# Summing seven taps on TensorE: row tiles with a short stream in place of column tiles

## The chip, the cores and the metric

The kernel runs on one core of a Trainium2 chip. Times are device microseconds (us) of one execution. The kernel before takes 418.44 us, the median of 3 runs (417.84 to 418.45); its profiled execution spans 416.7 us.

## What is computed

The input `x` has 8 sequences of 4160 tokens with 192 channels. Each token has, for each of 8 heads (24 channels), 7 weights. They go through a softmax, and each channel of the token becomes the weighted sum of that channel over the token and the six before it. The result goes through a layer of 1024 hidden values, each the larger of two products, and back to 192 channels.

```python
w = np.exp(weight_gen - max)                       # over the 7 taps
w = w / (np.sum(w, axis=-1, keepdims=True) + 1e-09)
out = np.einsum('bshk,bskhg->bshg', w, x_unf)      # x_unf: the token and the 6 before it
...
h1 = x @ w1                                        # 192 -> 1024
h2 = x @ w2
g = np.maximum(h1, h2)
return (g @ w_out).astype(np.float32)              # 1024 -> 192
```

## The kernel before

The 33280 tokens are laid on 128 partitions, 260 on each. Position number c on all partitions together, 128 tokens, is called a column here. Columns go in batches of 16, and each batch in pieces: four of 4 columns in the first two batches, two of 8 later. The first 32 columns are thus eight units of 4 columns.

For each piece ScalarE makes the softmax weights in bf16, each one twice, in the order tap, token, head:

```python
def weights(b, o):
    N = dict(pieces(b))[o] * H                     # 4 columns x 8 heads = 32
    ...
    nc.scalar.activation(
        out=_sub(en_ts[b], o * WGC * 2, [[2 * N, K], [2, N], [1, 2]]),
        in_=_sub(wg_ts[b], o * WGC, [[1, K], [K, N], [0, 2]]), func=AF.Exp,
    )
```

VectorE multiplies all seven taps of a piece in one instruction. The tile `m_t` then holds seven stretches (taps) of 4 x 192 products for each partition:

```python
def mul(b, o):
    n = dict(pieces(b))[o]
    nc.vector.tensor_tensor(
        out=m_t[:, K * o * D:K * (o + n) * D],
        in0=_sub(xb_ts[b], o * D, [[D, K], [1, n * D]]),
        in1=_sub(en_ts[b], o * WGC * 2, [[2, K * n * H], [0, G // 2], [1, 2]]),
        op=ALU.mult,
    )
```

For later columns VectorE adds up the taps and a DMA transposes the sum, so that channels stand on partitions. In the first 32 columns TensorE does both at once. Each product takes a block of `m_t` as its weights and the identity as its stream, which transposes the block, and the products of the taps add up in PSUM. In five of the eight units VectorE has added three pairs of taps before, so that four are left (`LEFT`); in three units all seven are summed here.

```python
def sum_transpose(u, taps=range(K)):
    b, o, n = UNITS[u]
    nb = n // 2 * 3                                # 6 blocks
    yps = ps[...].tile([P, 1024], FP32, name="yps", tag="op")
    for k in range(nb):
        for t in taps:
            for j in range(2):
                at = (K * o + t * n + k // 3 + j * n // 2) * D + k % 3 * 64
                nc.tensor.matmul(
                    yps[half(j), k * P:(k + 1) * P], lhsT=m_t[:, at:at + 64],
                    rhs=ident, start=(t == taps[0]), stop=(t == taps[-1]), skip_group_check=True,
                )
    yt = pyt.tile([P, 8 // 2 * 3 * P], BF16, name="yt", tag="yt")
    nc.scalar.copy(out=yt[:, 0:nb * P], in_=yps[:, 0:nb * P])
    yt_ts[u] = yt
```

A product has 128 tokens x 64 channels as weights and 128 columns of the identity as its stream. The two products `j` go to the two halves of the PSUM partitions: two column tiles of the array.

The result `yt` feeds the hidden layer (`hid_tile`, weights `wd`, tile `hdp` or `hd`), whose products have 64 rows and 128 columns, two row tiles. ScalarE rectifies it to bf16 (`relu`, tile `rd_t`), and the output products (`op_ps`) follow in two passes (`out_first`, with the terms of `yt` in it, and `out_second`). ScalarE copies their result to `o_t` (`evac`). An empty instruction on ScalarE's queue (`relay`) waits for the first pass and lets the second one start. A group is worked through like this:

```python
def hidden(g, now=(), between=lambda: None, beside=lambda: None):
    ...
    for t in range(t0, t0 + n - 1):
        hid_tile(t)
    if now:
        out_room(now, ...)
        last = out_first(now)
    ...                                            # relu of the first tiles
    if now:
        go = relay(last)
    hid_tile(t0 + n - 1)
    ...
    relu(rd, t0 + n - 1, 1)
    between()                                      # in groups 4 to 7: a sum_transpose
    if now:
        out_second(now, go)
        evac(now[0] // 2, len(now) // 2)
```

The eight sums stand in this order among other work: units 0 and 1 around the first groups, unit 2 before the fourth, unit 3 after it, each behind ScalarE's and VectorE's work of the opening; units 4 to 7 in groups 4 to 7. The pieces of weights of the first batch are made in a row at the start, those of the second batch in two pairs, ahead of the copy of unit 2 and behind that of unit 3.

Of the kernel before, what the change touches and what calls it, by code (L numbers as in the profile page):

```python
# [12 lines left out]
AF = mybir.ActivationFunctionType  # L13
# [4 lines left out]
def _sub(base: bass.AP, off: int, dims):  # L18
    ap = [list(base.ap[0])] + [[int(s), int(c)] for s, c in dims]
    return dataclasses.replace(base, offset=base.offset + off, ap=ap)  # L20
# [3 lines left out]
def kernel(  # L24
# [9 lines left out]
    nc = tc.nc  # L34

    B, S, D = x.shape
    H, K = weight_gen.shape[2], weight_gen.shape[3]
    F = moe_w1.shape[1]
    P = 128
    PAD = K - 1  # L40
    WGC = H * K
# [11 lines left out]
    def pieces(b):  # L53
        n = BATCHES[b][1]
        at, done = [], 0
        for w in (4, 4, 4, 4) if b < 2 else (8, 8) if n == 16 else (n,):
            at.append((done, w))
            done += w
        return at
# [38 lines left out]
    wg_ts, xb_ts, e_ts, s_ts, en_ts, y_ts, yt_ts = {}, {}, {}, {}, {}, {}, {}  # L98

    m_t = pm.tile([P, K * 16 * D], BF16, name="m_t")  # L100
# [48 lines left out]

    def weights(b, o):  # L150

        N = dict(pieces(b))[o] * H
        if b not in en_ts:
            en_ts[b] = pen.tile([P, 16 * WGC * 2], BF16, name="en_t", tag="en")
        nc.scalar.activation(  # L155
            out=_sub(en_ts[b], o * WGC * 2, [[2 * N, K], [2, N], [1, 2]]),
            in_=_sub(wg_ts[b], o * WGC, [[1, K], [K, N], [0, 2]]), func=AF.Exp,
        )


    def mul(b, o):

        n = dict(pieces(b))[o]
        nc.vector.tensor_tensor(  # L164
            out=m_t[:, K * o * D:K * (o + n) * D],
            in0=_sub(xb_ts[b], o * D, [[D, K], [1, n * D]]),
            in1=_sub(en_ts[b], o * WGC * 2, [[2, K * n * H], [0, G // 2], [1, 2]]),
            op=ALU.mult,
        )
# [44 lines left out]
    def half(j):  # L214
        return slice(64 * j, 64 * j + 64)
# [4 lines left out]
    def sum_transpose(u, taps=range(K)):  # L220

        b, o, n = UNITS[u]
        nb = n // 2 * 3
        yps = ps["r" if "r" in ps else "o"].tile([P, 1024], FP32, name="yps", tag="op")
        for k in range(nb):
            for t in taps:
                for j in range(2):
                    at = (K * o + t * n + k // 3 + j * n // 2) * D + k % 3 * 64
                    nc.tensor.matmul(  # L229
                        yps[half(j), k * P:(k + 1) * P], lhsT=m_t[:, at:at + 64],  # L230
                        rhs=ident, start=(t == taps[0]), stop=(t == taps[-1]), skip_group_check=True,
                    )
        yt = pyt.tile([P, 8 // 2 * 3 * P], BF16, name="yt", tag="yt")
        nc.scalar.copy(out=yt[:, 0:nb * P], in_=yps[:, 0:nb * P])
        yt_ts[u] = yt


# [143 lines left out]
    for g in range(3, len(GROUPS)):  # L381
        most = 4 if g == 3 else 2 if GROUPS[g][1] == 2 or len(OUTS[-1]) == 4 else 4
        n = min(most, ready[g] - c)
# [75 lines left out]
    ident = consts.tile([P, P], BF16, name="ident")  # L459
# [4 lines left out]
    with tc.tile_pool(name="pstage", bufs=1) as pstage:  # L464
# [7 lines left out]
        for p0, p1, eng in ((16, P, nc.sync), (1, 16, nc.gpsimd)):  # L472
            eng.dma_start(
                out=xs[p0:p1, 0:PAD * D],
                in_=bass.AP(tensor=x.tensor, offset=(p0 * CPP - PAD) * D,
                            ap=[[CPP * D, p1 - p0], [1, PAD * D]]),
# [38 lines left out]
        for o in (0, 4, 8, 12):  # L515
            weights(0, o)
        nc.vector.tensor_copy(out=xb_ts[0][:, PAD * D:(PAD + 4) * D],
                              in_=xs[:, PAD * D:(PAD + 4) * D])
        mul(0, 0)
        nc.scalar.copy(out=xb_ts[0][:, (PAD + 4) * D:(PAD + 8) * D], in_=xs[:, (PAD + 4) * D:])  # L520
        w1 = {kind: pstage.tile([nr, F], BF16, name="w1" + kind)
              for kind, nr in (("E", P), ("T", 64))}

        def w_diff(h, copy):
# [15 lines left out]
            out=wo[:, :].rearrange("p (f d) -> p f d", d=D),  # L540
            in_=bass.AP(tensor=moe_w_out.tensor, offset=0, ap=[[D, P], [P * D, FCH], [1, D]]),
# [29 lines left out]
        keep_warm(115)  # L571
        w_diff(0, nc.scalar.copy)
        sum_transpose(0)
        keep_warm(14)
        mul(0, 4)


        nc.scalar.copy(out=w1["E"], in_=ws["E", 0])
        hidden(0)
        nc.scalar.copy(out=w1["T"], in_=ws["T", 0])  # L580
        w_diff(1, nc.vector.tensor_copy)
        mul(0, 8)
        adds(0, 8, True)
        sum_transpose(1)
        exp_sum(1)
        red(1)
# [24 lines left out]
        for h in range(2):  # L611
            nc.scalar.copy(out=w1t[:, 4 * h * D:4 * (h + 1) * D], in_=tp[:, h * 1024:h * 1024 + 4 * D])
        weights(1, 0)
        weights(1, 4)
        mul(1, 0)
        adds(1, 0, True)
        sum_transpose(2, LEFT)
        load_x(2, 0, 16)
        load_wg(4, nc.gpsimd)
# [111 lines left out]
```

The softmax here doesn't subtract the row's maximum and nothing guards it: scores larger than these inputs give would overflow.

## Time and profile before

| | before |
|---|---|
| time, median of 3 | 418.44 us |
| span of the profiled execution | 416.7 us |
| TensorE busy | 402.9 us (97%) |
| VectorE busy | 377.3 us (91%) |
| ScalarE busy | 360.1 us (86%) |
| products of `sum_transpose` | 492, from 11.9 to 53 us |
| granted TensorE clock | full in all stretches up to 395 us |

PE is TensorE (PEld its weight loads, which run beside the matmuls), DVE VectorE, ACT ScalarE, POOL GpSimd, SP SyncE; L229 is line 229 of the kernel before. In that kernel L229 is the product of `sum_transpose` and L234 the copy of its sum, L155 the exponentials in `weights`, L164 the multiply, L181, L187 and L190 the additions on VectorE, L261 the hidden layer, L271 its rectification, L301 and L313 the output products, L357 the copy of their result, L127 the first exponential and L334 the empty instruction. A line of a group gives the engine, the operation, the tiles, the shape, the count, busy time and mean nanoseconds of one, and then the idle time just before, with what ended it. A line of the timeline gives start and duration in us, engine, line, tiles and count; brackets hold the idle time before it. Matmuls overlap, so the time of one (220 ns) is not the time that one costs in a row of many.

### The profile page before, as it was taken

How to read it: one execution, taken by the hardware profiler on the slowest of the kernel's cores; microseconds unless marked ns; L12 is line 12 of the kernel's file. 1: busy time of each engine (PE TensorE's matmuls, PEld its weight loads, DVE VectorE, ACT ScalarE, POOL GpSimd, SP SyncE). 2: the span in 40 equal slices, each digit the busy share in tenths (PEclk: the TensorE clock that was granted, in tenths of full speed). 3: DMA queues.
4: the chain of work that ended last, by engine and by line, in shares of the span. 5: the costliest groups of instructions: out<-in, count | busy, mean ns of one | idle time of the engine just before them, and what ended most of it. 6: DMA issues, size and time to landing. Idle time of an engine off the chain costs nothing.

```text
span 416.7 us, 15916 instructions
## 1 busy us (share of the span) xinstructions
PE 402.9 (97%) x7369; PEld 326.2 (78%) x7369; DVE 377.3 (91%) x218; ACT 360.1 (86%) x416; POOL 69.2 (17%) x102
## 2 busy tenths in 40 slices
PE   7899999999999999999999999999999999999995
PEld 7878899777777778777777777777778777787795
DVE  5999999999999999999999999999999999997000
ACT  5798989999999899898989989899898998887781
POOL 1410101221210222112111212222013220200000
PEclk9999999999999999999999999999999999999999
DMA  8965426865568766985966687666877576474213
GB/s 238 256 168 171 109 69 169 182 155 127 134 161 182 187 156 135 232 150 141 213 144 160 171 170 197 141 172 183 134 215 112 152 182 153 115 164 131 82 68 125
DMA packets 60242, 65.68 MB, mean 158 GB/s; under 512 B 47601, under 2 KB 48497, under 8 KB 60176
## 3 DMA queue, kind: packets, MB, share of 16 engines
q0 software_dynamic: 8128, 24.11, 28.2%
q1 hardware_dynamic: 46720, 15.30, 21.3%
q10 hardware_dynamic: 5328, 25.27, 15.6%
q8 instruction: 57, 0.93, 0.9%
q14 instruction: 9, 0.07, 0.1%
HBM read 35.96 MB, written 25.56 MB: 148 GB/s over the span
## 4 chain that ended last, share of the span: by engine, by line
PE 73%; ACT 14%; DVE 5%; issue 3%; DMA 2%; SPq 1%; ACTq 0%; DVEq 0%
PE op_ps L301 34%; PE hd L261 31%; ACT rd_t L271 8%; PE op_ps L313 7%; ACT en_t L155 3%; DVE m_t L164 2%; DMA xs<-in_x_dram 2%; ACT o_t L357 2%; PE yps L229 1%; PE hdp L261 1%; DVE m_t L181 1%; ACT e_t L127 1%; SPq L491 1%; ACTq L367 0%; DVE m_t L187 0%
## 5 line engine op out<-in xcount | busy, mean ns | idle before, releaser
L271 ACT ACTIVATE rd_t<-hd 128x1024 bf16<-128x1024 f32 (+1 forms) x206 | 234.5, 1183 | 28.5 <-PE hd L261 28.1
L301 PE MATMUL op_ps<-wo,rd_t 64*128 64x192 bf16 x4160 | 210.3, 243 | 0.1
L301 PEld LDWEIGHTS <-rd_t 64*128 64x128 bf16 x4160 | 180.1, 94 | 16.2 <-ACTq L334 0.3
L261 PE MATMUL hd<-yt,wd 64*128 64x512 bf16 (+1 forms) x1584 | 187.2, 360 | 0.9 <-ACT rd_t L271 0.9
L164 DVE TENSOR_TENSOR m_t<-xb_t,en_t 128x10752 bf16<-128x10752 bf16 (+1 forms) x37 | 187.6, 5071 | 0.4 <-ACT en_t L155 0.2
L261 PEld LDWEIGHTS <-wd 64*128 64x128 bf16 x1776 | 92.8, 94 | 42.7 <-issue 2.2
L205 POOL CAST gate<-yt 128x1 f32<-128x1 bf16 x29 | 34.2, 1179 | 278.4 <-DMA yt<-y_t 278.4
L181 DVE TENSOR_TENSOR m_t<-m_t 128x4608 bf16<-128x4608 bf16 (+1 forms) x34 | 79.5, 2339 | 0.1
L357 ACT COPY o_t<-op_ps 128x384 f32<-128x384 f32 (+1 forms) x99 | 57.1, 587 | 8.2 <-PE op_ps L301 8.1
L313 PE MATMUL op_ps<-w,yt 64*128 64x192 bf16 x780 | 55.3, 243 | 3.0 <-ACT o_t L357 2.2
L313 PEld LDWEIGHTS <-yt 64*128 64x128 bf16 x780 | 38.5, 94 | 19.8 <-issue 5.0
L187 DVE TENSOR_TENSOR m_t<-m_t 128x3072 bf16<-128x3072 bf16 (+1 forms) x29 | 50.0, 1724 | 0.1
L155 ACT ACTIVATE en_t<-wg_t 128x896 bf16<-128x896 f32 (+1 forms) x37 | 34.1, 936 | 1.9 <-ACT o_t L357 1.2
L190 DVE TENSOR_TENSOR y_t<-m_t 128x1536 bf16<-128x1536 bf16 (+1 forms) x29 | 27.3, 942 | 0.5
L347 DVE COPY o_t<-op_ps 128x192 f32<-128x192 f32 x1 | 0.4, 358 | 28.8 <-ACT o_t L347 28.8
L147 DVE TENSOR_TENSOR wg_t<-wg_t,sum_t 128x280 f32<-128x280 f32 (+4 forms) x45 | 22.0, 489 | 1.2 <-ACT sum_t L142 1.0
L139 DVE TENSOR_REDUCE sum_t<-e_t 128x64 f32<-128x448 f32 (+2 forms) x30 | 19.6, 653 | 2.7 <-ACT e_t L127 2.7
L115 POOL DMA_DIRECT2D xb_t<-in_x_dram x32 | 17.2, 539 | 24.4 <-DVE m_t L164 15.6
L127 ACT ACTIVATE e_t<-wg_t 128x896 f32<-128x896 f32 (+1 forms) x17 | 15.8, 928 | 3.1 <-DMA wg_t<-in_weight_gen_dram 2.6
L271 ACT ACTIVATE rd_t<-hdp 128x1024 bf16<-128x1024 f32 x16 | 15.7, 1027 | 1.5 <-PE hdp L261 0.5
L229 PE MATMUL yps<-ident,m_t 128*64 128x128 bf16 x492 | 15.3, 220 | 0.8 <-DVE m_t L164 0.7
L229 PEld LDWEIGHTS <-m_t 128*64 128x64 bf16 x492 | 14.1, 110 | 2.4 <-issue 1.5
(45 smaller groups left out, 83.4 us busy)
## 6 DMA issues: line engine op xcount, KB each, us to landing
out_dram<-o_t ACTq DMA_DIRECT2D x28, 768.0 KB, 3.9
xb_t<-in_x_dram POOLq DMA_DIRECT2D x28, 384.0 KB, 5.1
wg_t<-in_weight_gen_dram POOLq DMA_DIRECT2D x14, 448.0 KB, 5.8
xb_t<-xb_t POOLq DMA_DIRECT2D x16, 288.0 KB, 5.7
out_dram<-o_t ACTq DMA_DIRECT2D x8, 384.0 KB, 2.7
wg_t<-in_weight_gen_dram SPq DMA_DIRECT2D x2, 448.0 KB, 5.1
xs<-in_x_dram SPq DMA_DIRECT2D x2, 384.0 KB, 6.9
xb_t<-in_x_dram POOLq DMA_DIRECT2D x1, 768.0 KB, 6.8
```

What stands on the lines that cost most here:

```text
L155: nc.scalar.activation(out=_sub(en_ts[b], o * WGC * 2, [[2 * N, K], [2, N], [1, 2]]), in_=_sub(wg_ts[b], o * WGC, [[1, K], [K, N], [0, 2]] ...
L164: nc.vector.tensor_tensor(out=m_t[:, K * o * D:K * (o + n) * D], in0=_sub(xb_ts[b], o * D, [[D, K], [1, n * D]]), in1=_sub(en_ts[b], o * W ...
L181: nc.vector.tensor_tensor(out=taps(0, 1, 3), in0=taps(0, 1, 3), in1=taps(3, 1, 3), op=ALU.add)
L187: nc.vector.tensor_tensor(out=taps(0, 2, 2), in0=taps(0, 2, 2), in1=taps(1, 5, 2), op=ALU.add)
L190: nc.vector.tensor_tensor(out=_sub(y_ts[b], o * D, [[64, 2], [P, 3 * w // 2], [1, 64]]), in0=taps(0, 1, 1), in1=taps(2, 1, 1), op=ALU.add,)
L205: nc.gpsimd.tensor_copy(out=gate, in_=yt[:, 0:1])
L229: nc.tensor.matmul(yps[half(j), k * P:(k + 1) * P], lhsT=m_t[:, at:at + 64], rhs=ident, start=(t == taps[0]), stop=(t == taps[-1]), skip_g ...
L261: nc.tensor.matmul(hid_out(t, f, j), lhsT=wd[half(j), s * F + f * P:s * F + (f + 1) * P], rhs=_sub(yt_ts[u][half(j), :], (s + j) % 3 * P, ...
L271: nc.scalar.activation(out=rd[:, k * 1024:(k + n) * 1024], in_=hd[:, at:at + n * 1024], func=AF.Relu)
L301: return nc.tensor.matmul(op_out(c), lhsT=rd[half(r), k * 1024 + at:k * 1024 + at + P], rhs=wo[half(r), f * D:(f + 1) * D], start=False, s ...
L313: nc.tensor.matmul(op_out(c + j), lhsT=yt_ts[u][half(j), (3 * i + (s + j) % 3) * P:(3 * i + (s + j) % 3 + 1) * P], rhs=w10[half(j), s * D: ...
L357: nc.scalar.copy(out=_sub(o, c % 24 * D, [[D, len(qs)], [h * D, 2], [1, D]]), in_=_sub(tile_, at + (qs[0] - p) * D, [[D, len(qs)], [512, 2 ...
```

## The change

The taps are still summed on TensorE with the same number of products, but each product now takes 64 tokens (half of the partitions) x 128 channels as weights and streams only the 64 columns of the identity that belong to these tokens. The two products `r` of a pair use the two row tiles, as the layers around them do, and write to two PSUM banks. The stream of a product is half as long, and no other tiling stands between those of the neighbours.

For that the 128 channels of a block must lie side by side in `m_t`: 64 of one column and 64 of the column two further on. So the multiply writes in runs of 64, first the two lower columns of a piece and then the two upper ones, and the weights must stand in that order too: two activations of half the size, one for each pair of columns. The copy of the sum puts the two banks back into the old order of `yt`. Later batches keep the old form of weights and multiply.

```diff
     def weights(b, o):
 
-        N = dict(pieces(b))[o] * H
+        w = dict(pieces(b))[o]
...
-        nc.scalar.activation(
-            out=_sub(en_ts[b], o * WGC * 2, [[2 * N, K], [2, N], [1, 2]]),
-            in_=_sub(wg_ts[b], o * WGC, [[1, K], [K, N], [0, 2]]), func=AF.Exp,
-        )
+        J = 2 if w == 4 and b < 2 else 1
+        N = w * H // J
+        for j in range(J):
+            nc.scalar.activation(
+                out=_sub(en_ts[b], (o * WGC + j * N * K) * 2, [[2 * N, K], [2, N], [1, 2]]),
+                in_=_sub(wg_ts[b], (o * H + j * N) * K, [[1, K], [K, N], [0, 2]]), func=AF.Exp,
+            )
 
     def mul(b, o):
 
         n = dict(pieces(b))[o]
+        if n == 4 and b < 2:
+            m_out = _sub(m_t, K * o * D, [[64, 2], [P, K * 6], [1, 64]])
+            x_in = _sub(xb_ts[b], o * D, [[2 * D, 2], [D, K], [1, 2 * D]])
+        else:
+            m_out = m_t[:, K * o * D:K * (o + n) * D]
+            x_in = _sub(xb_ts[b], o * D, [[D, K], [1, n * D]])
         nc.vector.tensor_tensor(
-            out=m_t[:, K * o * D:K * (o + n) * D],
-            in0=_sub(xb_ts[b], o * D, [[D, K], [1, n * D]]),
+            out=m_out, in0=x_in,
...
     def sum_transpose(u, taps=range(K)):
...
-        for k in range(nb):
+        for k in range(6):
             for t in taps:
-                for j in range(2):
-                    at = (K * o + t * n + k // 3 + j * n // 2) * D + k % 3 * 64
+                for r in range(2):
+                    at = (K * o + t * n) * D + k * P
                     nc.tensor.matmul(
-                        yps[half(j), k * P:(k + 1) * P], lhsT=m_t[:, at:at + 64],
-                        rhs=ident, start=(t == taps[0]), stop=(t == taps[-1]), skip_group_check=True,
+                        yps[:, r * 512 + k * 64:r * 512 + (k + 1) * 64],
+                        lhsT=m_t[half(r), at:at + P], rhs=ident[half(r), half(r)],
+                        start=(k == 0 and t == taps[0]), stop=(t == taps[-1]),
+                        skip_group_check=True,
                     )
         yt = pyt.tile([P, 8 // 2 * 3 * P], BF16, name="yt", tag="yt")
-        nc.scalar.copy(out=yt[:, 0:nb * P], in_=yps[:, 0:nb * P])
+        nc.scalar.copy(out=_sub(yt, 0, [[64, 2], [P, 6], [1, 64]]),
+                       in_=_sub(yps, 0, [[512, 2], [64, 6], [1, 64]]))
```

More of the change, by code (lines that the diff above doesn't have):

```diff
@@ L222, in sum_transpose @@
         b, o, n = UNITS[u]
-        nb = n // 2 * 3
+        assert n == 4
         yps = ps["r" if "r" in ps else "o"].tile([P, 1024], FP32, name="yps", tag="op")
-        for k in range(nb):
+        for k in range(6):
             for t in taps:
-                for j in range(2):
-                    at = (K * o + t * n + k // 3 + j * n // 2) * D + k % 3 * 64
+                for r in range(2):
+                    at = (K * o + t * n) * D + k * P
                     nc.tensor.matmul(
-                        yps[half(j), k * P:(k + 1) * P], lhsT=m_t[:, at:at + 64],
-                        rhs=ident, start=(t == taps[0]), stop=(t == taps[-1]), skip_group_check=True,
+                        yps[:, r * 512 + k * 64:r * 512 + (k + 1) * 64],
+                        lhsT=m_t[half(r), at:at + P], rhs=ident[half(r), half(r)],
+                        start=(k == 0 and t == taps[0]), stop=(t == taps[-1]),
+                        skip_group_check=True,
                     )
         yt = pyt.tile([P, 8 // 2 * 3 * P], BF16, name="yt", tag="yt")
-        nc.scalar.copy(out=yt[:, 0:nb * P], in_=yps[:, 0:nb * P])
+        nc.scalar.copy(out=_sub(yt, 0, [[64, 2], [P, 6], [1, 64]]),
+                       in_=_sub(yps, 0, [[512, 2], [64, 6], [1, 64]]))
         yt_ts[u] = yt
```

## The prediction, made before the changed kernel ran

> **What bounds the kernel now.** I read the table of the engines first, then the same figures by stretch of time, then the chain that ended last in order of time, and last the instructions of the opening one by one.
>
> ```profile
> PE 402.9 (97%) x7369; PEld 326.2 (78%) x7369; DVE 377.3 (91%) x218; ACT 360.1 (86%) x416; POOL 69.2 (17%) x102
> ...
> L229 PE MATMUL yps<-ident,m_t 128*64 128x128 bf16 x492 | 15.3, 220 | 0.8 <-DVE m_t L164 0.7
> ```
>
> The products to be changed are 492 instructions, all of the first 53 us, and TensorE is busy with them for 15.3 us of 402.9. That is the most that could be touched: 3.7% of the span. By stretch (start and end, length, then busy time and instructions of PE, PEld, DVE, ACT, POOL):
>
> ```profile
> 12.00:24.00 12.00, 11.12 (x269) 9.80 (x269) 11.46 (x11) 10.94 (x14) 4.54 (x8) 1.00 1.16 248
> 24.00:34.40 10.40, 9.28 (x222) 8.08 (x216) 10.22 (x5) 10.37 (x19) 1.60 (x3) 1.00 0.64 138
> 34.40:58.00 23.60, 23.54 (x560) 21.47 (x562) 23.60 (x14) 19.42 (x27) 1.06 (x2) 1.00 0.39 116
> ```
>
> From 24 to 34.4 ScalarE is full (10.37 of 10.40); from 34.4 to 58 TensorE is full (23.54 of 23.60) and ScalarE has 4.2 us to spare. After 58 TensorE waits for 3.1 us in all until the end. The chain in order of time agrees:
>
> ```profile
> 27.33 1.02 ACT en_t L155 x2
> ...
> 33.81 0.57 ACT en_t L155 x2
> 34.42 1.49 PE op_ps L301 x32
> ...
> 38.13 1.46 PE yps L229 x48
> ...
> 51.68 1.46 PE yps L229 x48
> ```
>
> So of the eight sums only the last four, of 48 products each, lie on the chain. The first four, at 11.9, 17.3, 24.2 and 29.1 us, end in copies by ScalarE that stand in its queue behind other work anyway. The weights (L155) are on the chain twice, before 34.4. But "TensorE is full" hides a second limit. ScalarE's instructions from 37.7 us on:
>
> ```profile
> 37.73 1.94 ACT L271 ACTIVATE rd_t<-hdp 128x1024 bf16<-128x1024 f32 x2 [0.45 <-PE op_ps L301]
> 39.63 0.80 ACT L234 CAST yt<-yps 128x768 bf16<-128x768 f32 x1
> 40.40 0.48 ACT L357 COPY o_t<-op_ps 128x384 f32<-128x384 f32 x1
> 40.78 0.95 ACT L127 ACTIVATE e_t<-wg_t 128x896 f32<-128x896 f32 x1
> 41.63 1.02 ACT L155 ACTIVATE en_t<-wg_t 128x896 bf16<-128x896 f32 x1
> 42.54 1.94 ACT L271 ACTIVATE rd_t<-hdp 128x1024 bf16<-128x1024 f32 x2
> 44.35 0.82 ACT L234 CAST yt<-yps 128x768 bf16<-128x768 f32 x1
> 45.02 0.52 ACT L357 COPY o_t<-op_ps 128x384 f32<-128x384 f32 x1
> ...
> 53.19 0.80 ACT L234 CAST yt<-yps 128x768 bf16<-128x768 f32 x1 [0.44 <-PE yps L229]
> ```
>
> No bracket, no wait: from 37.73 to 45.5 us ScalarE has no gap, and TensorE's work is only just ready for it. Not until 53.19 does a copy wait for a sum.
>
> **What the Trainium skill says.** "TensorE: Matmul & The Clock Gate", section "Wait — 56ns, not 53.3ns?": a stream of N columns costs N/2.4 ns plus about 2.5, and starts never follow closer than about 25 ns. The trace agrees with the first part. The sum of 48 takes 1.53 us with matmuls of 0.22, so 23 pair periods in 1.31 us, 57 ns a pair for 128 columns (formula 56). L301 with 192 columns: 16 in 0.82 us, (0.82-0.24)/7 = 83 ns a pair (82.5). Eight transposes of the expert weights with 64 columns, one after the other, take 0.40 us with matmuls of 0.19: 30 ns each (29.2). Pairs on two tiles thus share one period. Whether the floor of 25 ns counts for a pair or for each product, no row here shows: products now come 28 ns apart on average.
>
> "TensorEngine Tiling (Array Packing)", section "Key Properties": changing the tiling mode drains TensorE. The trace agrees. Before the sum at 38.06, the last pair of L261 (12 matmuls from 37.31 for 0.82, each 0.27) starts at 37.86; the next was due 0.11 later, and starts at 38.06: 0.09 lost. After it L301 starts at 39.53, where 39.43 was due: 0.10 lost. "TensorE: Matmul & The Clock Gate", section "Weight-path perf modes — Fast Weight Load (FWL) and DoubleRow": fast loads need 128 weight columns. In the trace the first four loads of L301 (64x128) take 0.11 us, each 0.09, and the first four of a sum (128x64) 0.14 us, each 0.11: about 15 against 30 ns between two pairs of loads.
>
> "VectorE: DVE Perf Modes", section "What auto-detection actually checks": two-byte operands of step one keep the doubled rate. The trace has a write in runs of 64 already: L190, 1536 elements in 942 ns. L164 gives 5.75 us for 10752 and 2.95 for 5376, so 156 ns plus 0.52 ns an element; for 1536 that is 955. Runs of 64 cost nothing.
>
> **The change part by part.** *Products.* Their number stays (84 a sum with seven taps, 48 with four). A pair now streams 64 columns on two row tiles: 29 ns instead of 57 if pairs stay the unit. A sum of 48 goes from 1.53 us to 23 x 29 + 190 = 0.86 us. The row tiles are the mode of L261 and L301 on either side, so the two drains, 0.19 us, go too. On TensorE's own time a sum of four taps saves 24 x 28 + 190 = 0.86 us, one of seven 42 x 28 + 190 = 1.37.
>
> *VectorE.* The eight multiplies write runs of 64 in the other order: no change, 2.95 us each.
>
> *Copy of the sum.* It reads two banks in runs of 64. L357 reads two banks in pieces for 768 elements in 0.80 us, as the copy of now does: no change.
>
> *Weights.* Each of the eight pieces becomes two activations of half the size. Four pieces in a row take 2.13 us, each 0.615: one starts 0.505 after the other. With 896 columns the next starts 0.91 later (41.63 to 42.54). So 0.90 ns an element plus about 0.1; half a piece takes 0.31 and two halves 0.62: 0.11 us more for each piece. The four of the start (8.2 to 10.4) fall before a wait of ScalarE of 1.95 us for x. Only the first delays the multiply behind it, by 0.1 us, and of that almost nothing is left, as the next multiply waits for x until 13.17 anyway. The four pieces at 27.2 and 33.7 are on the chain: 0.44 us. TensorE's second pass at 34.42 waits for an empty instruction on ScalarE's queue, which is released when the last activation has started. Its start moves by 0.22 for the first two pieces, and then from 33.71+0.52 to 33.71+3 x 0.31: together 0.63 us.
>
> *Where it goes.* Everything from 34.4 is 0.63 us later. ScalarE without a gap carries that unchanged to 45.5 whatever TensorE saves: the output products of the next group wait for the copy of the sum before, and that copy starts at 40.26 and 44.98. The gains of the sums at 38.1, 42.5 and 47.0 turn into waits of TensorE, save about 0.2 us where ScalarE itself waited for it. At the products of 49.94 TensorE is still some 0.45 us behind. The last sum, at 51.6, is free: 0.45 - 0.86 gives -0.4. The rectification ahead of it, which ends at 53.2 and gives the next group its banks, takes 0.1 of that. After 58 TensorE carries what is left to the end: VectorE's results for columns from 32 on land 10.6 us before their first use at 75.7 and more than 11 us before at the end. Sum: -0.3 us.
>
> **The rivals.** *No pairs: each product keeps at least 25 ns.* For it speaks the floor above, and that four instructions would have to issue in 29 ns where now they have 57. Against it: the two starts of a pair lie a few ns apart now. A sum then loses the drains and 3 ns a product, 0.3 us for 48; the last sum no longer outruns the delay: +0.45-0.3 and a little, about +0.2 to +0.4 us.
>
> *TensorE's gain goes through in full.* If ScalarE were not the limit from 37.7 to 45.5, four sums would give 3.4 us less 0.6: 415.6. Against it stands the unbroken row of ScalarE above.
>
> *The multiplies lose their doubled rate*: 2.8 us on each of eight, of which two lie ahead of 24 us, and the rest uses up the 10.6 us that VectorE is ahead: 425 to 430. L190 speaks against it.
>
> *Halves dearer than 0.31 us* (rows of 32 values have more steps): with 0.36 each, 0.2 to 0.4 us more.
>
> **Range and chances.** About 0.55 for pairs (-0.3), 0.35 for the floor (+0.3), 0.1 for the others, so nearly nothing on average: 418.4. Runs of the kernel before lie 0.6 us apart, and that, with the share of the full gain, sets the range 417.0 to 419.6. Neither 2% limit, 8.4 us, is in reach of anything but the slow multiply: 0.01 faster, 0.97 same, 0.02 slower.
>
> **What would show it.** The sum of 48 near 0.85 us (floor: 1.2 to 1.35); L229's matmuls shorter, its loads 64x128; no lost time on either side. The multiplies at 2.95. Weights at half size 0.31 us apart. The second pass at 35.0 rather than 34.4. ScalarE without gaps to 46, and new waits of L313 for the copy L234 or of L261 for L271 between 40 and 51 us. Wrong it would be if TensorE had no new waits there, or the time fell under 417 or rose over 420.

## The result and the profile after

The changed kernel takes 417.32 us (median of 4 runs, 416.65 to 418.47) against 418.27 for the kernel before beside it: a ratio of 0.9983, interval 0.9964 to 1.0002. Measured again twice, with 21 and 22 runs, it gave 0.9988 (0.9975 to 1.0001) and 0.9983 (0.9972 to 0.9993). By the ratios it is 0.5 to 0.7 us faster, by the medians 0.7 to 1.1: about 0.2%. Two of the three intervals still contain 1. The prediction was 418.4 us, with -0.3 us for the change in its likeliest case.

In the changed kernel the product of the sum is L237, its copy L244, the weights L158, the hidden layer L272 with its rectification L282, and the output products L312 and L324. The table of engines and the clock row of the page, changed kernel:

```profile
PE 398.3 (96%) x7369; PEld 323.7 (78%) x7369; DVE 377.2 (91%) x218; ACT 360.4 (86%) x424; POOL 74.4 (18%) x102
...
PEclk9989999999999999999999999999999999999999
```

TensorE is busy 4.6 us less with as many instructions. VectorE is unchanged. ScalarE has eight instructions more, the halved weights. In the clock row the third digit is new; in the kernel before the clock was full there.

The group of products and of copies, changed kernel (minimum, median and maximum of one in ns, then the first and last start):

```profile
L237 PE MATMUL yps<-ident,m_t x492: 187/190/258, 12.4 to 53.2; 64*128 64x64 bf16 x164
L244 ACT CAST yt<-yps x8: 778/798/833, 14.2 to 53.6; 128x768 bf16<-128x768 f32 x8
```

The products now stream 64 columns, and the copy costs 0.80 us as before. TensorE in order of time, in groups 4 to 7:

```profile
38.74 0.82 PE L272 MATMUL hdp<-yt,wd 64*128 64x256 bf16 x12
39.39 0.86 PE L237 MATMUL yps<-ident,m_t 64*128 64x64 bf16 x48
40.09 0.82 PE L312 MATMUL op_ps<-wo,rd_t 64*128 64x192 bf16 x16
...
46.28 0.42 PE L324 MATMUL op_ps<-w,yt 64*128 64x192 bf16 x6 [0.77 <-ACT yt L244]
...
50.94 0.42 PE L324 MATMUL op_ps<-w,yt 64*128 64x192 bf16 x6 [0.91 <-ACT yt L244]
...
53.86 1.49 PE L272 MATMUL hd<-yt,wd 64*128 64x256 bf16 x24
```

A sum of 48 takes 0.86 us, so a pair comes every (0.86-0.19)/23 = 29.1 ns. The sums of 84 take 1.40: (1.40-0.19)/41 = 29.5 ns. The sum starts where the hidden layer's next pair was due, and L312 follows 0.70 us after it; in the kernel before it was 1.47, in TensorE's timeline there:

```profile
38.06 1.53 PE L229 MATMUL yps<-ident,m_t 128*64 128x128 bf16 x48
39.53 0.83 PE L301 MATMUL op_ps<-wo,rd_t 64*128 64x192 bf16 x16
```

The two brackets of the changed kernel are the new waits for the copy of the sum before. ScalarE in the same stretch, changed kernel:

```profile
38.94 1.94 ACT L282 ACTIVATE rd_t<-hdp 128x1024 bf16<-128x1024 f32 x2 [0.45 <-PE op_ps L312]
40.76 0.81 ACT L244 CAST yt<-yps 128x768 bf16<-128x768 f32 x1
41.44 0.51 ACT L368 COPY o_t<-op_ps 128x384 f32<-128x384 f32 x1
...
43.59 1.95 ACT L282 ACTIVATE rd_t<-hdp 128x1024 bf16<-128x1024 f32 x2
45.40 0.83 ACT L244 CAST yt<-yps 128x768 bf16<-128x768 f32 x1
```

It is again without a gap. The opening of this execution is different, though. TensorE in order of time, changed kernel:

```profile
19.88 0.51 PE L567 MATMUL tp<-ident,w1E 128*128 128x128 bf16 x6
22.67 0.37 PE L567 MATMUL tp<-ident,w1E 128*128 128x128 bf16 x2 [2.28 <-issue]
```

The windows of that stretch (start and end, length, busy time and instructions of PE, PEld, DVE, ACT and POOL, and then the granted clock, the DMA share and GB/s):

```profile
20.40:22.60 2.20, 0.00 (x0) 0.00 (x0) 2.17 (x3) 2.20 (x3) 0.00 (x0) 1.00 0.99 289
22.60:26.10 3.50, 3.43 (x45) 3.11 (x45) 3.12 (x3) 1.74 (x3) 0.00 (x0) 0.51 0.89 239
26.10:34.00 7.90, 5.30 (x178) 4.70 (x174) 6.37 (x4) 7.78 (x16) 1.60 (x3) 1.00 0.60 99
```

TensorE stands for 2.28 us between two transposes of the expert weights and waits for nothing that the profile names. Then its clock is 0.51 for 3.5 us. Before, the same place cost 0.17 us at full clock. A 16 KB load of instructions starts at 20.32 us in the same stretch, with the transfer engines 99% busy. The second output pass starts at 35.84, where it was 34.42. This execution took 418.47 us, the slowest of the four.

To compare profiles with different openings I use three spans of each: the start of the second output pass; from there to the end of TensorE's last matmul; and from there to the end of the kernel (the tail). Times are medians in us; the spans come from the one profiled execution of each, so they need not add up to the median. "Late" are the sums of units 4 to 7, "early" those of 0 to 3.

| kernel | time | ratio (interval) | second pass | to the last matmul | tail |
|---|---|---|---|---|---|
| before | 418.2 to 418.3 | | 34.42 | 377.31 | 4.97 |
| after | 417.32 | 0.9983 (0.9964 to 1.0002) | 35.84 | 376.35 | 4.50 |
| again, 1 | 417.55 | 0.9988 (0.9975 to 1.0001) | 34.34 | 376.47 | 4.50 |
| again, 2 | 417.10 | 0.9983 (0.9972 to 0.9993) | 34.29 | 376.77 | 4.49 |
| new order, old tiles | 418.25 | 1.0002 (0.9993 to 1.0012) | 34.56 | 377.39 | 4.50 |
| long warm-up | 418.56 | 1.0018 (1.0002 to 1.0033) | 34.51 | 376.40 | 6.03 |
| order by the subtraction | 418.69 | 1.0011 (0.9999 to 1.0023) | 34.68 | 377.17 | 4.95 |
| late sums only | 417.11 | 0.9967 (0.9953 to 0.9980) | 34.33 | 377.80 | 4.49 |
| late sums only, again | 417.17 | 0.9988 (0.9964 to 1.0011) | 34.04 | 376.80 | 4.49 |
| early sums only | 418.16 | 1.0002 (0.9989 to 1.0015) | 34.20 | 377.29 | 4.50 |
| lighter ScalarE, after | 417.18 | 0.9974 (0.9964 to 0.9984) | 34.65 | 376.40 | 4.50 |
| lighter ScalarE, before | 418.36 | 1.0010 (0.9995 to 1.0024) | 34.31 | 377.29 | 4.96 |
| lighter, seven taps | 418.91 | 1.0017 (1.0005 to 1.0029) | 34.45 | 376.99 | 4.49 |
| late sums, seven taps | 418.39 | 1.0002 (0.9990 to 1.0015) | 34.10 | 377.03 | 4.49 |

### The profile page after: what moved, and what is told of

The parts are those of the page before. It is cut to its first block, busy times and chain, and to the rows that moved or that the text cites. A ratio compares the mean times of both kernels' runs of the same rounds, so it can differ in the third digit from the quotient of the medians.

```text
span 416.7 us, 15924 instructions
## 1 busy us (share of the span) xinstructions
PE 398.3 (96%) x7369; PEld 323.7 (78%) x7369; DVE 377.2 (91%) x218; ACT 360.4 (86%) x424; POOL 74.4 (18%) x102
## 4 chain that ended last, share of the span: by engine, by line
PE 74%; ACT 18%; issue 4%; DMA 2%; SPq 1%; ACTq 1%; DVE 0%; DVEq 0%
PE op_ps L312 34%; PE hd L272 31%; ACT rd_t L282 10%; PE op_ps L324 7%; ACT en_t L158 3%; PE hdp L272 2%; ACT o_t L368 2%; DMA ws1T<-in_moe_w_dram 2%; ACT e_t L127 1%; ACT yt L244 1%; ACTq L378 0%; PE yps L237 0%; SPq L502 0%; ACT w1t L623 0%; ACT w L617 0%
## 5 line engine op out<-in xcount | busy, mean ns | idle before, releaser
L282 ACT ACTIVATE rd_t<-hd 128x1024 bf16<-128x1024 f32 (+1 forms) x206 | 234.4, 1183 | 28.1 <-PE hd L272 27.6
L312 PE MATMUL op_ps<-wo,rd_t 64*128 64x192 bf16 x4160 | 210.6, 243 | 0.1
L312 PEld LDWEIGHTS <-rd_t 64*128 64x128 bf16 x4160 | 180.4, 94 | 15.9 <-ACTq L345 0.3
L272 PE MATMUL hd<-yt,wd 64*128 64x512 bf16 (+1 forms) x1584 | 187.4, 360 | 0.9 <-ACT rd_t L282 0.9
L272 PEld LDWEIGHTS <-wd 64*128 64x128 bf16 x1776 | 95.3, 95 | 42.1 <-issue 2.7
L213 POOL CAST gate<-yt 128x1 f32<-128x1 bf16 x29 | 38.7, 1335 | 274.6 <-DMA yt<-y_t 274.6
L324 PE MATMUL op_ps<-w,yt 64*128 64x192 bf16 x780 | 55.5, 243 | 5.7 <-ACT o_t L368 2.2
L324 PEld LDWEIGHTS <-yt 64*128 64x128 bf16 x780 | 38.7, 94 | 23.0 <-issue 8.7
L158 ACT ACTIVATE en_t<-wg_t 128x896 bf16<-128x896 f32 (+2 forms) x45 | 34.8, 803 | 2.2 <-ACT o_t L368 1.7
L282 ACT ACTIVATE rd_t<-hdp 128x1024 bf16<-128x1024 f32 x16 | 15.9, 1029 | 3.6 <-PE hdp L272 2.8
L272 PE MATMUL hdp<-yt,wd 64*128 64x256 bf16 x192 | 14.2, 288 | 1.1 <-issue 0.7
L579 PE MATMUL warm<-ident 128*128 128x128 bf16 x129 | 10.4, 260 | 3.0 <-DVE ident L518 3.0
```

Source lines behind the costliest of these rows:

```text
L158: nc.scalar.activation(out=_sub(en_ts[b], (o * WGC + j * N * K) * 2, [[2 * N, K], [2, N], [1, 2]]), in_=_sub(wg_ts[b], (o * H + j * N) * K ...
L213: nc.gpsimd.tensor_copy(out=gate, in_=yt[:, 0:1])
L272: nc.tensor.matmul(hid_out(t, f, j), lhsT=wd[half(j), s * F + f * P:s * F + (f + 1) * P], rhs=_sub(yt_ts[u][half(j), :], (s + j) % 3 * P, ...
L282: nc.scalar.activation(out=rd[:, k * 1024:(k + n) * 1024], in_=hd[:, at:at + n * 1024], func=AF.Relu)
L312: return nc.tensor.matmul(op_out(c), lhsT=rd[half(r), k * 1024 + at:k * 1024 + at + P], rhs=wo[half(r), f * D:(f + 1) * D], start=False, s ...
L324: nc.tensor.matmul(op_out(c + j), lhsT=yt_ts[u][half(j), (3 * i + (s + j) % 3) * P:(3 * i + (s + j) % 3 + 1) * P], rhs=w10[half(j), s * D: ...
```

## The experiments

### The changed kernel once more

No edit. Was the clock behind the spread of the first runs?

> The changed kernel once more. Theory A: what it takes depends on TensorE's clock in the opening. Where TensorE stands still at about 20.4 us (2.3 us in the first profile, waiting for nothing that the profile shows, while one load of 16 KB of instructions runs among saturated DMA engines), its clock is halved from 22.6 to 26.1 and ScalarE's copies start 1.2 us later. Runs with a mean clock of 0.998 or more then take 416.5 to 416.9, runs with 0.994 to 0.995 take 417.8 to 418.6, and nothing in between. A profile without the halving has the second output pass at 34.6 to 35.1 us (35.85 with it). Rival B: the spread comes from later on, from transfers; then the times do not sort by the mean clock.

Measured: 417.55 us over 21 runs, spread from 416.8 to 418.5 with values all the way between. TensorE in its opening, this run:

```profile
19.50 0.51 PE L567 MATMUL tp<-ident,w1E 128*128 128x128 bf16 x6
22.17 0.27 PE L567 MATMUL tp<-ident,w1E 128*128 128x128 bf16 x2 [2.16 <-issue]
...
33.40 2.44 PE L312 MATMUL op_ps<-wo,rd_t 64*128 64x192 bf16 x48
```

Here TensorE stood for 2.16 us, the clock stayed full, and the second pass began at 34.34: this standstill cost nothing, because ScalarE carries the opening. By this comparison it was the half clock that moved the first profile's opening by 1.4 us. "TensorE: Matmul & The Clock Gate", section "What's actually happening", in the Trainium skill says that an idle window of about 3.4 us halves the clock; here 2.28 us of standing were enough once, and 2.16 were not. But two heaps of run times with nothing between were expected, and there is a smear. The mean clock of each execution does sort the long ones: of the 47 of the changed kernel in all three measurements, the 17 that took 417.8 us or more all have 0.996 or less, and the 24 with 0.998 or more took 416.65 to 417.69. But four of at most 0.996 took 416.8 to 417.1, so the clock is one cause of the spread and not all of it.

### New order, old column tiles

The weights in halves and the new order of `m_t`, but the old products and copy:

```diff
-                    at = (K * o + t * n + k // 3 + j * n // 2) * D + k % 3 * 64
+                    at = (K * o + t * n) * D + k * P + j * 64
```

> The new order of the products of the taps and the half-size weights, but summed as before, in column tiles that stream 128 columns. It has the cost of the change without its gain. By the prediction ScalarE's halves delay the second output pass by 0.63 us (from 34.42 to 35.05) and nothing makes up for it: 418.7 to 419.0 where the kernel before takes 418.2, multiplies at 2.95 us. Rival: the halves cost nothing because the ScalarE row has slack ahead of 34.4 us: 418.2 to 418.3. No standstill of TensorE over 1 us and no halved clock before 40 us, as the sums take as long as before.

Measured: 418.25 us, 1.0002 (0.9993 to 1.0012), so the preparation by itself costs nothing that can be measured. Its timeline of TensorE:

```profile
33.62 2.44 PE L309 MATMUL op_ps<-wo,rd_t 64*128 64x192 bf16 x48
...
38.21 1.53 PE L237 MATMUL yps<-ident,m_t 128*64 128x128 bf16 x48
```

And of ScalarE:

```profile
27.18 1.32 ACT L158 ACTIVATE en_t<-wg_t 128x224 bf16<-128x224 f32 x4
...
33.85 1.30 ACT L158 ACTIVATE en_t<-wg_t 128x224 bf16<-128x224 f32 x4
```

Four half pieces take 1.30 to 1.32 us, where two whole ones took 1.12 to 1.15: 0.09 us for each piece. The second pass starts at 34.56, 0.14 later than before, and not 0.63. From the start of the first pass to that of the second it is 2.1 us here as in the kernel before (32.47 to 34.56, 32.32 to 34.42). The empty instruction runs at 34.50, before the last of the four halves starts at 34.75. The pieces ahead of the second pass do not hold it; only the first two, which delay the first pass, count. And the late sums run in 1.53 us: the whole gain of the changed kernel up to the last matmul, 0.6 to 1.0 us against this run, comes from the row tiles with their shorter stream.

### Fewer instructions in the warm-up

Does TensorE stand still because its instructions arrive too slowly? The products that warm its clock in the opening were made four times as long, and their number cut from 129 to 33:

```diff
-                nc.tensor.matmul(warm[:, 0:P], lhsT=ident, rhs=ident, start=True, stop=True,
-                                 skip_group_check=True)
+                nc.tensor.matmul(warm[:, 0:4 * P], lhsT=ident, rhs=_sub(ident, 0, [[0, 4], [1, P]]),
+                                 start=True, stop=True, skip_group_check=True)
-        keep_warm(115)
+        keep_warm(29)
-        keep_warm(14)
+        keep_warm(4)
```

> The changed kernel, with the warm-up products of the opening in the same time but with 512 columns each: 33 products instead of 129, 192 instructions fewer ahead of the first groups. Theory A (TensorE runs through its instructions faster than they are loaded in the opening): the standstill at the eight transposes of the expert weights (2.3 us) goes or moves behind the opening, the clock is not halved, mean clock 0.998 or more in every run, 416.5 to 416.9. Rival: the standstill belongs to the place (the transposes, the transfers of the opening) and not to the count of instructions: it stays at about 20.4 us, and the times stay as spread as in the changed kernel.

Measured: up to 60 us no standstill without a named cause is left on TensorE, and the clock is full. But the time is 418.56 us, slower than the changed kernel. The last matmul ends at 410.91, and the end comes 6.03 us later. The last two issues of stores, in the timeline of this run:

```profile
411.30 1.13 ACTq L359 DMA_DIRECT2D out_dram<-o_t  x1
...
411.74 0.73 SPq L359 DMA_DIRECT2D out_dram<-o_t  x1
```

They take 1.13 and 0.73 us; in the changed kernel each takes 0.34. The list of transfers shows a 16 KB load of instructions from 410.10 us on. So the standstill is tied to the number of instructions, and taking it away gained nothing, since ScalarE holds that stretch; the shifted loads met the end instead.

The traces of all 14 profiles together say what kind of tie it is. Beyond 0.15 us TensorE stands still without a named cause 20 times in them. Counted in its matmuls and weight loads from the start, this is after 448, 704, 1218, 1986 or 3010 of them, which lie multiples of 256 apart to within two. The changed kernel has 57 loads of 16 KB of this kind for its 14738 matmuls and weight loads, one for 259. And in all 20 cases TensorE goes on 1.2 to 1.5 us after such a load has ended. This is what a wait for the next block of instructions would look like; no run changed the loads by themselves.

This sent me to the tail of the other kernels. The list of transfers of the kernel before, from 411 us to the end (a queue with its kind, packets, MB and share of time; a store with its size and the us from issue to landing):

```profile
q14 instruction: 1, 0.01, 0.3%
...
out_dram<-o_t SPq DMA_DIRECT2D x1, 96.0 KB, 2.8
```

The same of the changed kernel:

```profile
out_dram<-o_t SPq DMA_DIRECT2D x1, 96.0 KB, 2.3
```

Before, an instruction load of another queue (8 KB) falls beside the last store, which takes 2.8 us to land. In the changed kernel the load comes before 408 us, and the same store lands in 2.3. This holds in all profiles: with 416 instructions on ScalarE (before, the lighter kernel before, and the one with the order by the subtraction) the load falls after 411.5 us and the tail is 4.95 to 4.97; with 420 or 424 it falls earlier and the tail is 4.49 to 4.50, but for the long warm-up. So 0.46 us of the gain in the profiles goes with a load of instructions that the added activations moved off the end. That this load is what delays the store is inferred from its place; no run moved it by itself. How much of the 0.46 us reaches the medians isn't shown either: the new order with old tiles has the shorter tail and no gain before it, and its median is 0.03 us over that of the kernel before (418.25 and 418.22).

### The order made by the subtraction

The first two batches keep one activation for each piece; VectorE's subtraction of the log of the sum writes the new order:

```diff
+        if b < 2:
+            nc.vector.tensor_tensor(
+                out=_sub(e_ts[b], 0, [[2 * H * K, 8], [1, 2 * H], [2 * H, K]]),
+                in0=_sub(wg_ts[b], 0, [[2 * H * K, 8], [K, 2 * H], [1, K]]),
+                in1=_sub(s_ts[b], 0, [[2 * H, 8], [1, 2 * H], [0, K]]), op=ALU.subtract)
```

> The changed kernel without half-size weights: the subtraction on VectorE that precedes them (L147, 1.09 us, first two batches) writes its result in the new order into the tile of the first exponential, and one activation a piece reads it in one run. If the halves cost 0.63 us at the second output pass, this is 0.4 to 0.6 us faster than the changed kernel at the same clock (416.0 to 416.3 without the halving of the clock), the pieces start 0.50 us apart or less, and the subtraction stays near 1.1 us. If the strided write makes the subtraction slower (1.5 us or more), the two of the opening take that gain back.

Measured: 418.69 us. ScalarE's two pieces now take 1.04 us, in its timeline of this run:

```profile
33.97 1.04 ACT L163 ACTIVATE en_t<-e_t 128x448 bf16<-128x448 f32 x2
```

VectorE's subtraction takes 1.72 us instead of 1.09, in the groups of the opening (busy time, mean ns of one, and the idle time before it):

```profile
L148 DVE TENSOR_TENSOR e_t<-wg_t,sum_t 128x896 f32<-128x896 f32 x2 | 3.4, 1718 | 0.8 <-ACT sum_t L142 0.8
```

What ScalarE saves, VectorE spends, on a chain that runs through both: the second pass starts at 34.68, and TensorE waits for the copy of a sum once more than in the changed kernel, 0.62 us at 41.28. The halves are the cheaper way, the more so as without the eight activations the tail is 4.95 again.

### Only the late sums, only the early sums

The new form of weights, multiply and sum for one batch alone, the old form for the other:

```diff
-        J = 2 if w == 4 and b < 2 else 1
+        J = 2 if w == 4 and b == 1 else 1
-        if n == 4 and b < 2:
+        if n == 4 and b == 1:
```

(and the same choice in `sum_transpose`; the other kernel has `b == 0`).

> Only the last four sums (units 4 to 7) with their weights and multiplies in the new form; the first four as before. Theory A: only the last four lie on the path, so the whole gain over the order alone is here (TensorE's end 1.1 us earlier than with column tiles), and the opening is that of the kernel before, without a standstill of over 1 us and without a halved clock: 416.9 to 417.4, median 0.8 to 1.3 us under the kernel before, and runs within 0.4 us of each other like those of the kernel before, where the changed kernel spread from 416.8 to 418.5. Rival: the first four sums contribute too; then it stays at 417.6 or more.

> The other half: only units 0 to 3 in the new form, the last four sums in column tiles. Theory A: nothing to gain, and the standstill of TensorE at 20 us stays, with the halved clock in part of the runs: 418.0 to 419.5, a median not under that of the kernel before, and more spread than there. Rival: half of the gain of the changed kernel, 417.8 or less.

Measured: late only 417.11 us, 0.9967 (0.9953 to 0.9980); early only 418.16, 1.0002 (0.9989 to 1.0015). From the second pass to the last matmul the early form changes 0.02 us. So all of the gain ahead of the tail lies in the last four sums, as the chain had said. The profiled execution of the late form was the slowest of its 13 (418.43), and its timeline shows why its span to the last matmul is long:

```profile
36.59 1.25 PE L326 MATMUL op_ps<-wo,rd_t 64*128 64x192 bf16 x26 [1.84 <-issue]
```

Again a standstill with a 16 KB load of instructions ahead of it, at 34.28 us, now where TensorE is the limit. The ratio of 0.9967 looked like a version that beats the changed kernel, so both were run side by side:

> The changed kernel beside the next three, on the same chip: 416.8 to 418.6, median 417.3 to 417.7, about 0.7 us under the kernel before.

> The kernel with only the last four sums in the new form, again: median 416.9 to 417.3, 0.2 to 0.6 us under the changed kernel, with runs closer together than its. Rival: its lead over the changed kernel was chance between two calls; then both have the same median within 0.2 us.

Measured: 417.10 and 417.17 us, 0.9983 and 0.9988. The medians are equal, and the lead was a difference between two occasions. The late form alone is steadier, though: of its 22 executions none has a mean clock of 0.996 or less, and 20 took 416.69 to 417.55 us (the other two 418.43 and 422.11). The standstill at the transposes was 1.38 us with early and late sums on row tiles and 0.66 with the late ones alone.

### ScalarE relieved

Is ScalarE what holds back the gains of the first three late sums? Two kernels leave work out: the first exponential of batch 3 for all but one column in sixteen, and the weights of the first half of batch 2 for all but one tap. GpSimd fills the gaps with constants. Once on the changed kernel and once on the kernel before:

```diff
-        nc.scalar.activation(out=e_ts[b], in_=wg_ts[b], func=AF.Exp)
+        m = WGC if b == 3 else BATCHES[b][1] * WGC
+        nc.scalar.activation(out=e_ts[b][:, 0:m], in_=wg_ts[b][:, 0:m], func=AF.Exp)
+        T = 1 if b == 2 and o == 0 else K
```

> The changed kernel with 1.5 us less work for ScalarE between 40 and 44 us: the first exponential of batch 3 is made for one column in sixteen and the weights of the first half of batch 2 for one tap in seven (GpSimd, idle then, fills the rest with constants, so the work of all other engines stays). The prediction says that ScalarE without a gap holds back the gains of the sums at 38, 42.5 and 47 us; TensorE waits 1.7 us for ScalarE's copies of sums in groups 6 and 7. If so, these waits go and the time falls by 1.0 to 1.6 us below the changed kernel: 415.7 to 416.5. Rival: TensorE or VectorE holds the path there anyway: no change, 416.8 to 418.5 as the changed kernel.

> The same lightening of ScalarE in the kernel before, where TensorE has no gap between 34.4 and 58 us: by the prediction nothing is gained, 418.0 to 418.4. Rival: ScalarE holds the kernel before there too: 0.5 us or more less.

Measured: 417.18 us, 0.9974 (0.9964 to 0.9984), and 418.36, 1.0010 (0.9995 to 1.0024). The kernel before gains nothing. The changed one gains less than expected. Its first wait for the copy is gone; the one of 0.9 us in the next group stays. At 62 us TensorE is 0.8 us further ahead than in the changed kernel; it keeps that to 287 us and all but 0.2 us of it to 340. VectorE, ScalarE and TensorE there, in the timeline of the relieved changed kernel:

```profile
340.24 0.44 DVE L150 TENSOR_TENSOR wg_t<-wg_t,sum_t 128x280 f32<-128x280 f32 x1
...
340.71 1.03 ACT L164 ACTIVATE en_t<-wg_t 128x896 bf16<-128x896 f32 x1 [1.09 <-DVE wg_t L150]
...
343.40 0.42 PE L330 MATMUL op_ps<-w,yt 64*128 64x192 bf16 x6 [0.61 <-ACT o_t L374]
```

The weights of the last batches wait for VectorE's subtraction, rectification and copy stand behind them in ScalarE's queue, and TensorE waits for the copy. The subtraction stands in VectorE's row of work, which is full and is 0.53 us earlier here than in the kernel before (340.77). So relief for ScalarE does reach TensorE, and a second limit takes it back. How far TensorE is ahead of the kernel before, by the start of the issues of the same stores, less the difference of the second pass (us; names as in the table above):

| at about | 62 us | 80 us | 287 us | 356 us | last store |
|---|---|---|---|---|---|
| after | 1.29 | 1.20 | 1.13 | 0.95 | 0.96 |
| again, 1 | 1.23 | 0.94 | 0.85 | 0.83 | 0.84 |
| again, 2 | 1.24 | 0.64 | 0.53 | 0.54 | 0.54 |
| late sums only, again | 1.29 | 1.30 | 1.33 | 0.51 | 0.51 |
| lighter ScalarE, after | 2.05 | 2.05 | 2.06 | 0.91 | 0.91 |

All but the relieved one leave the sums with 1.23 to 1.29 us, and all arrive with 0.5 to 1.0. They lose it in different places. In the second repeat of the changed kernel it is TensorE's instruction supply, by its timeline, with one 16 KB load of instructions among the transfers of 72.5 to 74 us:

```profile
73.75 0.83 PE L312 MATMUL op_ps<-wo,rd_t 64*128 64x192 bf16 x16 [0.43 <-issue]
```

With the late sums only, ScalarE gets ahead of a load of data:

```profile
288.27 0.95 ACT L127 ACTIVATE e_t<-wg_t 128x896 f32<-128x896 f32 x1 [0.59 <-DMA wg_t<-in_weight_gen_dram]
...
290.88 0.42 PE L338 MATMUL op_ps<-w,yt 64*128 64x192 bf16 x6 [0.36 <-ACT o_t L382]
```

That is about 0.5 of its 0.8 us; the rest, 0.29, goes at 328 us. There TensorE's next hidden layer waits for a transposed sum of VectorE (`yt<-y_t`), whose DMA lands at 328.23; the layer starts at 328.37.

### More taps on TensorE

If VectorE is that second limit, it should pay to take three of its additions away and sum units 4 to 6 over all seven taps on TensorE. Once on the relieved kernel, with the same work left out, and once, with the whole computation, on the one with late sums only:

```diff
-        adds(1, 0, True)
-        adds(1, 4, True)
-        adds(1, 8, True)
-        4: (lambda: sum_transpose(4, LEFT), lambda: (end_of_1(), weights(2, 0))),
-        5: (lambda: sum_transpose(5, LEFT), none),
-        6: (lambda: (weights(2, 8), ln(3), sum_transpose(6, LEFT)), lambda: load_x(3, 0, 8)),
+        4: (lambda: sum_transpose(4), lambda: (end_of_1(), weights(2, 0))),
+        5: (lambda: sum_transpose(5), none),
+        6: (lambda: (weights(2, 8), ln(3), sum_transpose(6)), lambda: load_x(3, 0, 8)),
```

> The changed kernel with ScalarE lightened as before (the exponential of batch 3 and the first weights of batch 2 left out for the most part), and besides VectorE spared three additions of 1.36 us: units 4 to 6 are summed over all seven taps on TensorE, 0.53 us more for it in each. Theory C: the gain of the lightening was lost at 340.7 us, where ScalarE's weights waited 1.1 us for VectorE's subtraction, since VectorE has been full from 16 us on and sets that time. With VectorE 4 us ahead this wait goes: 416.0 to 416.6, and TensorE's end 0.5 to 1.0 us before that of the lightened kernel. Rival: the loss came from something else (a load of instructions, a transfer); then about 417.2 or more, as the 1.6 us of products come on top.

> Only the last four sums in the new form, and units 4 to 6 over all seven taps on TensorE, without the three additions on VectorE; all of the computation is done. TensorE waits for ScalarE there for 1.7 us in two groups, so most of its additional 1.6 us is hidden, and VectorE is 4 us ahead. Theory: 416.7 to 417.4, the same as with four taps within 0.3 us, as ScalarE holds the stretch from 38 to 50 us and at 340 us has just no wait for VectorE. Rival: TensorE's products are on the path: 1 us or more slower than with four taps.

Measured: 418.91 us, 1.0017 (1.0005 to 1.0029), and 418.39, 1.0002 (0.9990 to 1.0015). Both are over 1 us slower than their models with four taps. On the relieved kernel the wait at 341 us is gone: its weights start at 340.97 without one. But this doesn't show that a faster VectorE lifts the limit. The subtraction starts at 340.01, only 0.23 us earlier than with four taps, for VectorE spends most of the 4 us that it was spared in waits for ScalarE, by its timeline:

```profile
62.64 0.62 DVE L142 TENSOR_REDUCE sum_t<-e_t 128x64 f32<-128x448 f32 x1 [1.37 <-ACT e_t L128]
...
100.13 0.45 DVE L150 TENSOR_TENSOR wg_t<-wg_t,sum_t 128x280 f32<-128x280 f32 x1 [1.88 <-ACT sum_t L145]
```

And ScalarE comes to these weights 1.3 us later than with four taps: the rectification ahead of them ends at 340.95 instead of 339.63. The 0.5 us that TensorE loses here after 287 us goes at 328 us, again to a transposed sum that lands late, at 328.84, by TensorE's timeline:

```profile
328.97 1.25 PE L278 MATMUL hd<-yt,wd 64*128 64x512 bf16 x10 [0.34 <-DMA yt<-y_t]
```

The three sums over seven taps cost more than they give. In TensorE's timeline of the relieved kernel the third of them is broken in two:

```profile
46.21 0.46 PE L243 MATMUL yps<-ident,m_t 64*128 64x64 bf16 x20
47.78 1.11 PE L243 MATMUL yps<-ident,m_t 64*128 64x64 bf16 x64 [1.11 <-issue]
```

And in that of the kernel with the whole computation:

```profile
46.15 0.47 PE L238 MATMUL yps<-ident,m_t 64*128 64x64 bf16 x20
48.02 1.11 PE L238 MATMUL yps<-ident,m_t 64*128 64x64 bf16 x64 [1.40 <-issue]
```

After 20 of 84 products TensorE stands for 1.1 and 1.4 us. In the second, a 16 KB load of instructions starts at 45.72 us and takes 0.94. Both profiles are of executions well under the median of their kernel (417.72 and 417.45 us), so most of the loss in the medians isn't in them and stays unexplained. No version that was run beats the changed kernel by its median.

## Why the prediction was right

The time, 417.32 us, lay within the range of 417.0 to 419.6, but near its lower end and 1.1 us under the 418.4 that was put first. The mechanism held for the sums and for ScalarE; the cost of the halves and the way to the end were wrong. By its own steps:

- **Pairs.** "A pair now streams 64 columns on two row tiles: 29 ns" was right: 29.1 and 29.5. A sum of 48 takes 0.86 us, as worked out, and no time is lost at its start or end. The rival with 25 ns for each product falls: the two products of a pair start 2 to 4 ns apart, so that products come 14.6 ns apart on average.
- **Multiplies and copy.** 2.94 to 2.96 and 0.80 us, as predicted; that rival falls too.
- **Halves.** Eight in a row take 2.49 us, 0.30 apart, and 0.09 more for each piece (predicted 0.11).
- **The step that was wrong** is "Its start moves by 0.22 for the first two pieces, and then from 33.71+0.52 to 33.71+3 x 0.31: together 0.63 us." With the new order alone it was 0.14. The first pass to the second is 2.1 us in both forms, and the empty instruction runs before the last activation starts, so it was not held by it. Of the two parts only the first is real, and it measured 0.14 where 0.22 was put.
- **ScalarE without a gap.** Right, and both waits appeared: 0.77 and 0.91 us for L244. TensorE was ahead at the products of group 7 by 0.42 us (50.94-35.84 against 49.94-34.42); the "about 0.2 us" of the sum was half of that. The last sum added the full 0.89, to 1.31.
- **"After 58 TensorE carries what is left to the end."** This failed too: 1.23 to 1.29 us leave the sums, and 0.5 to 1.0 arrive. The prediction looked at VectorE's results at the two ends of the run, where the trace has them 10.7 and 10.8 us early. In between, in the kernel before, the transposed sums come closer and closer: they land 1.1 us before TensorE's instruction that waits for them at 328.5 us, and 0.6 us before that at 362.7. In two of the runs above TensorE waited there. Besides, ScalarE's weights are tied to VectorE's subtraction, and loads of data and of instructions stand in the way.
- **Not foreseen:** the tail, 0.46 us shorter, and TensorE's instruction supply in the opening.

In one sum of measured terms: +0.14 for the halves, -1.26 for the sums, +0.3 to +0.8 given back, -0.46 in the tail, so -0.8 to -1.3 us by profiles; the medians show -0.7 to -1.1. In part the range was met by luck. The halves were put 0.5 us too dear and the gain of the sums some 0.3 too small, so that 1.1 us and not 0.3 leave that stretch; then a loss and a gain that were both not foreseen, 0.3 to 0.8 on the way and 0.46 in the tail, about cancel. The opening varies from run to run besides: once it cost 1.4 us with the clock halved. The full gain of 3.4 us that was a rival is refuted by the two waits, 1.68 us together.

What stays open: why TensorE waits for instructions longer in some executions, and how much each part of the spread from 416.7 to 418.5 weighs. That the standstills are waits for instructions is inferred from their places in the stream and in time.

## What to carry to other kernels

Products on row tiles that stream half as many columns cost half here, 29 instead of 57 ns a pair, and with neighbours of the same tiling the 0.09 to 0.10 us at each change of tiling go too; but only the part on the chain counts, here the last of four sums and what an unbroken ScalarE lets through. Before booking a gain to the end, look along the whole run for the next engine or load that is only just in time: "10 us ahead" at both ends of the run said nothing of the middle, where the same results were 0.6 to 1.1 us early. A burst of very short products can outrun the engine's own instructions, so count instructions as well as columns.

## What the runs showed of the hardware

- TensorE stood still 20 times in 14 profiles without a named wait, each time at one of a row of places that lie multiples of 256 matmuls and weight loads apart (within two), and went on 1.2 to 1.5 us after a 16 KB load of instructions had ended. At the transposes the standstills were 0.17 to 0.93 us with the early sums on column tiles (six profiles), and 1.3 to 2.3 with them on row tiles (seven). They were gone with 96 products and their weight loads fewer ahead of them.
- In these sums the two products of a pair on two row tiles start 2 to 4 ns apart, and pairs of 64 columns follow every 29 ns.
- A standstill of 2.28 us was followed once by 3.5 us at a clock of 0.51, and one of 2.16 us was not.
- A load of instructions near the last stores goes with a longer tail: 4.49 to 4.50 us without, 4.96 with one of 8 KB, 6.03 with one of 16 KB.
- Four or eight activations more on ScalarE went with a tail 0.46 us shorter in the profiles, where the load of 8 KB then fell earlier.
